# Five of 32 weight conversions moved into the first group's up projections, and the converted chunks of the second matrix stored by one request

## The chip, the cores and the metric

The kernel runs on one core of a Trainium2 chip. The metric is device time in microseconds (us) of one execution. The three runs of the kernel before took 1008.73, 1010.57 and 1010.68 us, median 1010.57 us.

## The reference, cut to what matters

```python
def reference(...):
    attn_out = _attn_ref(q, k, v)              # 4 x 8 heads x 576 x 64; keeps the 32 largest scores of each row
    x = attn_out.transpose(0, 2, 1, 3).reshape(2304, 512)
    h = x @ w_in                               # moe: 512 -> 2048
    g = np.maximum(h, 0.0) + alpha * np.minimum(h, 0.0)
    x = g @ w_out                              # 2048 -> 512
    return _moe2_ref(x, ...)                   # 8 experts, routed by w_gate, skip by w_skip
```

The inputs `w_in` and `w_out` arrive as 64-bit floats. The kernel reads them as pairs of 32-bit words and turns each weight into a high and a low 32-bit part, whose sum is the weight; every product of the two matrices is then three matmuls (high by high, high by low, low by high).

## The kernel before, in words

**Conversions.** Each matrix has 16 chunks of 128 x 512 weights: chunks 0 to 15 are of `w_in`, 16 to 31 of `w_out` (`convs`, line 285). `convert(i)` (line 287) takes the raw chunk (512 KB, loaded into half a `wr` buffer by `conv_load`, line 275) and issues three ScalarE (ACT) instructions, lines 297, 299 and 301. It hands back three later parts. `bits`, 4 slots on, is one VectorE (DVE) instruction of line 305, and then requests the raw chunk `i + 4`. `split`, 8 slots on, is two GpSimd (POOL) instructions, lines 311 and 112. `store`, 13 slots on, marks the chunk as converted and requests its store to DRAM on SP's queue, line 317 for `w_in` and 320 for `w_out` (there two requests, one for the high parts and one for the low, each in pieces of 512 bytes). The stores of chunks 28, 30 and 31 also call `fetch(0)`, `fetch(1)` and `fetch(2)` (line 322).

**Weights for the products.** `fetch(j)` (line 609) requests the 1 MB piece `j` of the converted weights from DRAM into a `wr` buffer, if `wr[j]` isn't held yet and its chunks are converted. There are three `wr` buffers, and the raw chunks use the same three, two chunks to a buffer (`cvtile`, line 266). A buffer is taken again when every instruction that reads it is done, and the request on SP's queue waits for that. `need(i)` (line 621) is called by the first product that uses piece `i`: it drops the pieces before `i` from `wr`, fetches `i` and `i + 1`, and a slot later `i + 2`.

**Order of the work.** Attention has 80 units (128 rows of a pair of heads; of five units of a pair the last has half the width). The loop of line 1277 makes one step `kx` per unit, in 14 slots. Line 23 (`STEP`) says what is issued in which slot: the fold of unit `kx + 1` on DVE (line 468) in slot 0; the values of unit `kx - 2` (line 569) and the scores of unit `kx + 2` (line 447) on TensorE (PE) in slot 1; copies of the scores by ACT (line 452) in slots 2 and 3; the DVE rounds (477, 480) in slots 2 to 8; the weights of the unit (510) in slots 10 and 11. The conversions and the MoE products come out of a list `todo`. Each slot adds a budget, and entries are issued while it is positive (`slot`, line 1113): a conversion costs 1.9, half an up projection of 128 features (six matmuls, line 644) 0.64. An entry that is a condition holds up all behind it. The budget of a step from `kx = 1` on is the cost of what is left divided by the steps until the next group is due, kept between 4.3 and 6.0, and half of it where the unit of half width comes next (lines 1293 to 1295).

**The first group.** `todo` begins with the first `EC` conversions (line 1140); `EC = 32`, all of them. At step 9, slot 8, the group of the first 256 rows is queued (`queue_moe`, line 1211): 16 up projections (features f0 to f15, 12 matmuls each), which use the pieces 0 to 7, two features each; then the downs (line 719) with the pieces 8 to 15. `queue_moe` mixes what is left in `convq` into this first group (lines 1237 to 1240): a conversion after every second entry, each behind the condition that the conversion two before it has been stored, at a cost of 0.5 instead of 1.9. With `EC = 32` nothing is left there. An up projection's result is taken from PSUM by ACT alone (663, 664) or, if issued in the slots 4 to 8 or among the last three, by ACT (686) and DVE (689).

Of the kernel before, what the change touches and what calls it, by code (L numbers as in the profile page):

```python
# [10 lines left out]
U16 = mybir.dt.uint16  # L11
AF = mybir.ActivationFunctionType
# [19 lines left out]
        (10, 0, "weights", 0), (10, -1, "evac", 2),  # L32
        (11, 0, "weights", 1)]
AHEAD = 4
EC = 32
PH = 6
RD = 3
WHOLE = ()
# [24 lines left out]
def kernel(  # L63
# [15 lines left out]
    nc = tc.nc  # L79
# [5 lines left out]
    KD = DM // 128  # L85
# [24 lines left out]
    def sub(o, a, b):  # L110

        behind_fold(nc.gpsimd.tensor_tensor(o, a, b, op=OP.subtract))  # L112
# [66 lines left out]
    for i in range(2):  # L179
        t = const.tile([128, 128], F32, name=f"vbd{i}")  # L180
# [41 lines left out]
    win_s = [dram.tile([128, 2, 2, 512], F32, name=f"win{j}") for j in range(KF // 2)]  # L222
    wout_s = [dram.tile([KD, 128, 8, 2, 128], F32, name=f"wout{j}") for j in range(KF // 8)]
# [42 lines left out]
    def cvtile(i):  # L266

        if i:
            return moe.tile([128, 1024], F32, name="cv", tag="g", bufs=8)
        if not ring:  # L270
            t = moe.tile([128, 16, 128], F32R, name="wr", tag="wr", bufs=3).rearrange("p a c -> p (a c)").bitcast(F32)
            ring.extend(t[:, h * 1024:(h + 1) * 1024] for h in range(2))
        return ring.pop(0)

    def conv_load(kind, f):
        raw = cvtile(0).bitcast(I32).rearrange("p (d f t) -> p d f t", d=4, t=2)
        if kind == 0:
            nc.sync.dma_start(
                raw.rearrange("p d f t -> p d (f t)"),
                win32[:, f * 256:(f + 1) * 256].rearrange("(d p) f -> p d f", p=128))  # L280
        else:
            nc.sync.dma_start(raw.rearrange("p d f t -> p (d f t)"), wout32[f * 128:(f + 1) * 128, :])
        raws[kind, f] = raw
# [3 lines left out]
    def convert(i):  # L287

        kind, f = convs[i]
        raw = raws.pop((kind, f))  # L290
        r2 = raw.rearrange("p d f t -> p (d f) t")
        hi, lo = r2[:, :, 1], r2[:, :, 0]
        hif = hi.bitcast(F32)
        w = cvtile(1).rearrange("p (a c) -> p a c", a=2)


        nc.scalar.activation(w[:, 0], hif, AF.Copy, scale=2.0 ** -112)
        t2 = w[:, 1].bitcast(U16).rearrange("p (c k) -> p c k", k=2)
        nc.scalar.activation(t2[:, :, 1].bitcast(mybir.dt.float16), hif, AF.Copy, scale=2.0 ** -60)
        top = raw.rearrange("p d f t -> p (d f t)").bitcast(U16).rearrange("p (c k) -> p c k", k=4)[:, :, 1]  # L300
        nc.scalar.activation(t2[:, :, 0], top, AF.Copy, scale=2.0 ** -13, bias=2.0 ** -14 - 0.5)

        def bits():
            t = w[:, 1].bitcast(I32)
            nc.vector.scalar_tensor_tensor(t, w[:, 0].bitcast(I32), 3, t, op0=OP.logical_shift_left,
                                           op1=OP.bitwise_or)
            if i + AHEAD < len(convs):
                conv_load(*convs[i + AHEAD])

        def split():  # L310
            nc.gpsimd.tensor_copy(w[:, 0].bitcast(F32R), w[:, 1])
            sub(w[:, 1].bitcast(F32R), w[:, 1], w[:, 0])

        def store():
            converted.add(i)
            if kind == 0:
                nc.sync.dma_start(win_s[f // 2][:, f % 2], w)
            else:
                for a in range(2):
                    nc.sync.dma_start(wout_s[f // 8][:, :, f % 8, a, :].rearrange("d p c -> p d c"),  # L320
                                      w[:, a].rearrange("p (d c) -> p d c", d=KD))
            if i in (28, 30, 31):
                fetch((28, 30, 31).index(i))

        if i == 0:
            return none + [bits, split] + none * (2 * CV) + [store]
        return none * (CV - 1 if i > 1 else 3 * CV) + [bits] + none * (CV - 1) + [split] + none * CV + [store]
# [281 lines left out]
    def fetch(j):  # L609
        if j < len(stream) and j not in wr and stream[j][1] in converted:  # L610
            wr[j] = wload(stream[j][0])
# [524 lines left out]
    def main(work, exact, hooks=(lambda: [], lambda: [], None)):  # L1136

        if not exact:
            convq.extend(lambda i=i: convert(i) for i in range(2 * KF))
            todo.extend((ECC, convq.pop(0)) for i in range(EC))  # L1140
            todo.insert(24, (0.5, late_consts))
            todo.insert(17, (0.5, late_loads))
# [68 lines left out]
        def queue_moe(wi):  # L1211
# [16 lines left out]
            if early[0]:  # L1228

                early[0] = False  # L1230
                mixed, k, n = [], EC, 0
                for p in parts:
# [107 lines left out]
    def place(n):  # L1340
        t = xtile(n).rearrange("p a n s -> p (a n s)")
        return t, [t[:, i * 2048:(i + 1) * 2048].rearrange("p (a c) -> p a c", a=2) for i in range(2)]
# [96 lines left out]
    t, two_ = place(0)  # L1439
# [3 lines left out]
    while todo or late or rowq:  # L1443
# [14 lines left out]
        if len(group[1]) == 2 and len(ups) == len(work) and gone > G2:  # L1458
            t, two_ = place(1)
# [168 lines left out]
```

## Time and profile before

| | |
|---|---|
| three runs | 1008.73, 1010.57, 1010.68 us |
| profiled execution, its own time | 1010.48 us |
| its span (first to last instruction) | 1008.7 us |
| busy: PE, DVE, ACT, POOL | 885.7, 797.6, 642.4, 399.1 us |
| mean granted clock of PE | 0.952 of full speed |

The profile is of one execution; times in it count from the first instruction. A busy share is the time in which an engine executes, not how well. The idle time in brackets in a timeline stands before the instruction named, with what ended it. The engines take their own instructions in order, so an instruction that waits holds up all behind it on that engine, and the same holds for SP's queue of transfers.

### The profile page before, as it was taken

The page shows a single profiled execution, that of the slowest core. Times are in us where ns is not written, and L with a number is a line of the kernel's source. Part 1 is how long each engine was busy: PE and PEld are TensorE (multiplying, and loading weights), DVE is VectorE, ACT ScalarE, POOL GpSimd, SP SyncE. Part 2 cuts the span into 40 slices and gives each one's busy share as a digit, 9 for nine tenths or more (in the row PEclk, how much of TensorE's full clock was granted, in tenths as well). Part 3 has the DMA queues.
Part 4 walks back from the last instruction along what each step waited for, and adds up shares of the span by engine and source line. Part 5 has one row for each costly group of instructions (what it writes and reads, how often), then busy time and mean ns, then how long its engine had stood idle before and what let it go on. Part 6 is the DMA issues. An engine that isn't in the chain of part 4 may idle for free. (4 is left out here: it accounts for less than half of the span.)

```text
span 1008.7 us, 21245 instructions
## 1 busy us (share of the span) xinstructions
PE 885.7 (88%) x7054; PEld 786.9 (78%) x7054; DVE 797.6 (79%) x2652; ACT 642.4 (64%) x1723; POOL 399.1 (40%) x608
## 2 busy tenths in 40 slices
PE   4345569999999999999999999999778989999995
PEld 2234458898999888999998899999668988987542
DVE  5999998999898799979987997999878532366410
ACT  7879768767865687588558857865456434365320
POOL 5866664522651254245213623541285134024100
PEclk9977579999999999999999999999797999999998
DMA  8978985776656566776656777665464679879993
GB/s 236 331 271 239 304 256 202 220 228 207 227 188 241 162 234 203 266 232 228 213 188 208 236 242 240 224 209 191 140 179 166 222 254 414 331 246 393 397 397 145
DMA packets 133319, 244.89 MB, mean 243 GB/s; under 512 B 58830, under 2 KB 91598, under 8 KB 116816
## 3 DMA queue, kind: packets, MB, share of 16 engines
q1 hardware_dynamic: 129824, 239.42, 70.0%
q0 software_dynamic: 2176, 3.73, 1.1%
q8 instruction: 58, 0.95, 0.4%
q14 instruction: 61, 0.50, 0.1%
q10 hardware_dynamic: 1200, 0.30, 0.1%
HBM read 215.00 MB, written 28.92 MB: 242 GB/s over the span
## 5 line engine op out<-in xcount | busy, mean ns | idle before, releaser
L644 PE MATMUL pm<-x,wr 128*128 128x256 f32 (+1 forms) x1536 | 245.6, 307 | 19.4 <-DVE ra L689 8.1
L719 PE MATMUL pm<-g,wr 128*128 128x256 f32 (+1 forms) x1536 | 235.5, 303 | 2.7 <-DVE ra L689 2.1
L644 PEld LDWEIGHTS pm<-x,wr 128*128 128x128 f32 x1536 | 213.3, 192 | 28.9 <-DVE ra L689 14.4
L719 PEld LDWEIGHTS pm<-g,wr 128*128 128x128 f32 x1536 | 208.8, 189 | 8.3 <-issue 4.0
L477 DVE MAX8 v<-F 128x8 f32<-128x72 f32 (+2 forms) x576 | 213.7, 407 | 1.2 <-issue 0.2
L112 POOL TENSOR_TENSOR g<-ra,g 128x256 fp32r<-128x256 f32 (+1 forms) x128 | 102.3, 820 | 150.2 <-DVE st L515 75.7
L510 DVE SCALAR_TENSOR_TENSOR Ex<-sb,v,Ex 128x577 f32<-128x577 f32 x144 | 130.9, 936 | 0.0
L480 DVE MATCH_REPLACE8 F<-v,F 128x72 f32<-128x72 f32 (+1 forms) x432 | 123.2, 291 | 0.0
L452 ACT ACTIVATE sb<-ps 128x288 f32<-128x288 f32 x224 | 80.2, 415 | 57.9 <-PE ps L447 46.2
L502 ACT ACTIVATE Ex<-sb,st 128x576 f32<-128x576 f32 x144 | 105.3, 782 | 0.1
L112 POOL TENSOR_TENSOR x<-xf,x 128x128 fp32r<-128x128 f32 (+1 forms) x80 | 40.2, 503 | 163.0 <-DVE st L515 113.9
L548 ACT ACTIVATE PT<-pt 128x512 f32<-128x512 f32 x144 | 86.9, 604 | 20.9 <-PE pt L536 20.2
L536 PE MATMUL pt<-ident,Ex 128*128 128x128 f32 x576 | 87.1, 284 | 4.3 <-ACT sb L452 4.3
L569 PE MATMUL px<-PT,vt 128*64 128x128 f32 (+1 forms) x1280 | 89.8, 288 | 0.0
L447 PE MATMUL ps<-kT,qT 64*128 64x288 f32 x576 | 80.2, 349 | 6.9 <-ACT kT L357 2.5
L689 DVE SCALAR_TENSOR_TENSOR ra<-ra,slope,pm 128x320 f32<-128x320 f32 (+1 forms) x69 | 35.5, 515 | 57.7 <-ACT ra L686 57.5
L569 PEld LDWEIGHTS px<-PT,vt 128*64 128x64 f32 x1280 | 70.6, 149 | 9.8 <-issue 2.0
L447 PEld LDWEIGHTS ps<-kT,qT 64*128 64x128 f32 x576 | 61.9, 212 | 20.6 <-issue 9.4
L536 PEld LDWEIGHTS pt<-ident,Ex 128*128 128x128 f32 x576 | 71.5, 147 | 6.7 <-ACT sb L452 6.0
L565 PE MATMUL px<-PT,vbd 128*128 128x128 f32 (+1 forms) x160 | 34.9, 302 | 39.3 <-ACT PT L553 37.4
L468 DVE TENSOR_TENSOR F<-m 128x144 f32<-128x144 f32 (+2 forms) x240 | 66.2, 329 | 0.0
L468 DVE TENSOR_TENSOR m<-sb 128x576 f32<-128x576 f32 (+1 forms) x80 | 64.8, 809 | 1.8 <-ACT sb L452 1.8
(379 smaller groups left out, 1558.9 us busy)
## 6 DMA issues: line engine op xcount, KB each, us to landing
wr<-win SPq DMA_DIRECT2D x64, 1024.0 KB, 5.0
wr<-wout SPq DMA_DIRECT2D x64, 1024.0 KB, 5.0
wd<-in_moe_w_dram SPq DMA_DIRECT2D x40, 512.0 KB, 11.4
wraw<-in_moe_w_dram SPq DMA_DIRECT2D x32, 512.0 KB, 7.1
wr<-in_moe_w_in_dram SPq DMA_DIRECT2D x16, 512.0 KB, 5.7
vt<-in_v_dram SPq DMA_DIRECT2D x32, 256.0 KB, 2.8
win<-cv SPq DMA_DIRECT2D x16, 512.0 KB, 4.9
wr<-in_moe_w_out_dram SPq DMA_DIRECT2D x16, 512.0 KB, 5.5
```

Source lines behind the costliest of these rows:

```text
L112: behind_fold(nc.gpsimd.tensor_tensor(o, a, b, op=OP.subtract))
L447: nc.tensor.matmul(self.ps[h, j][:, 0:HALF], lhsT=hd["q"][gp, a, u * 128 - hd["c0"]:(u + 1) * 128 - hd["c0"]], rhs=hd["k"][gp, b_, c0:c0 + ...
L468: gate[0] = nc.vector.tensor_tensor(o[:, n_], a[:, n_, 0:w], a[:, n_, w:2 * w], op=op)
L477: nc.vector.max(v8[:, h, r, :], F[:, h, 0:w])
L480: nc.vector.match_replace(out=F[:, h, 0:w], in_to_replace=v8[:, h, r, :], in_values=F[:, h, 0:w], imm_value=NEG)
L502: nc.scalar.activation(self.Ex[:, h, :], self.sb[:, h, :], AF.Exp, bias=self.st[:, 0, h:h + 1], scale=0.125)
L510: nc.vector.scalar_tensor_tensor(self.Exp[:, cs], self.sbp[:, cs], v8[:, h, 3, 7:8], self.Exp[:, cs], op0=OP.is_ge, op1=OP.mult, accum_out ...
L536: nc.tensor.transpose(pt[:, c * 128:(c + 1) * 128], P[:, c0:c0 + 128], ident)
L548: nc.scalar.activation(PT[:, 4 * h:4 * h + 4, :].rearrange("p a b -> p (a b)"), pt, AF.Copy)
L569: nc.tensor.matmul(x[h * 64:(h + 1) * 64, 0:n], lhsT=hd["vt"][:, h, c, :], rhs=rhs, start=False, stop=(c == SF - 1))
L644: nc.tensor.matmul(hp[:, 0:n], lhsT=w[:, (f % 2) * 8 + a * 4 + d, :], rhs=x[:, d, c0:c1], start=(i == 0), stop=(i == 3 * KD - 1))
L719: nc.tensor.matmul(op_[:, 0:n], lhsT=w[:, 2 * f + a, :], rhs=g[(hf + ch) * 8 + f, sg][:, gg, 0:n], start=(i == 0), stop=(i == ni - 1))
```

## The change

`EC` is 27: the conversions 27 to 31 (the last five chunks of `w_out`) are left in `convq`, and `queue_moe` mixes them in among the first up projections. A converted chunk of `w_out` is laid out with the high and low parts of each quarter side by side (the three ACT instructions, the one of DVE and the two of POOL address it in four runs), and stored by one request in pieces of 1 KB, in place of two requests in pieces of 512 bytes.

```diff
-EC = 32
+EC = 27
...
         kind, f = convs[i]
         raw = raws.pop((kind, f))
-        r2 = raw.rearrange("p d f t -> p (d f) t")
-        hi, lo = r2[:, :, 1], r2[:, :, 0]
+        hi = raw[:, :, :, 1]
         hif = hi.bitcast(F32)
-        w = cvtile(1).rearrange("p (a c) -> p a c", a=2)
+        t4 = cvtile(1)
+        w = t4.rearrange("p (d a c) -> p a d c" if kind else "p (a d c) -> p a d c", a=2, d=4)
...
-        t2 = w[:, 1].bitcast(U16).rearrange("p (c k) -> p c k", k=2)
-        nc.scalar.activation(t2[:, :, 1].bitcast(mybir.dt.float16), hif, AF.Copy, scale=2.0 ** -60)
-        top = raw.rearrange("p d f t -> p (d f t)").bitcast(U16).rearrange("p (c k) -> p c k", k=4)[:, :, 1]
-        nc.scalar.activation(t2[:, :, 0], top, AF.Copy, scale=2.0 ** -13, bias=2.0 ** -14 - 0.5)
+        t2 = w[:, 1].bitcast(U16).rearrange("p d (c k) -> p d c k", k=2)
+        nc.scalar.activation(t2[:, :, :, 1].bitcast(mybir.dt.float16), hif, AF.Copy, scale=2.0 ** -60)
+        top = raw.rearrange("p d f t -> p d (f t)").bitcast(U16).rearrange("p d (c k) -> p d c k", k=4)[:, :, :, 1]
+        nc.scalar.activation(t2[:, :, :, 0], top, AF.Copy, scale=2.0 ** -13, bias=2.0 ** -14 - 0.5)
...
             if kind == 0:
-                nc.sync.dma_start(win_s[f // 2][:, f % 2], w)
+                nc.sync.dma_start(win_s[f // 2][:, f % 2], t4.rearrange("p (a c) -> p a c", a=2))
             else:
-                for a in range(2):
-                    nc.sync.dma_start(wout_s[f // 8][:, :, f % 8, a, :].rearrange("d p c -> p d c"),
-                                      w[:, a].rearrange("p (d c) -> p d c", d=KD))
+                nc.sync.dma_start(wout_s[f // 8][:, :, f % 8].rearrange("d p a c -> p d a c"),
+                                  t4.rearrange("p (d a c) -> p d a c", a=2, d=4))
             if i in (28, 30, 31):
                 fetch((28, 30, 31).index(i))
```

## Rows read from the trace of the kernel before

**Rows 1.** Stages: window, length, busy (count) of PE, PEld, DVE, ACT, POOL, PEclk, DMA share, GB/s.
```profile
41.10:138.60 97.50, 51.15 (x313) 40.87 (x313) 97.47 (x281) 80.11 (x187) 64.89 (x70) 0.69 0.85 258
146.40:157.70 11.30, 10.88 (x78) 10.05 (x79) 8.47 (x34) 6.63 (x22) 2.89 (x7) 0.70 0.72 251
...
199.00:206.80 7.80, 7.80 (x79) 7.41 (x78) 7.80 (x31) 5.46 (x16) 2.13 (x5) 1.00 0.43 140
...
168.90:237.50 68.60, 65.57 (x622) 61.32 (x623) 67.66 (x248) 50.48 (x157) 27.06 (x47) 1.00 0.67 218
237.50:700.00 462.50, 452.46 (x3999) 426.02 (x3999) 421.20 (x1505) 329.02 (x959) 175.47 (x268) 1.00 0.66 219
```

**Rows 2.** Timeline of DVE: start, us, what. A step begins with m<-sb.
```profile
138.63 0.85 DVE L468 TENSOR_TENSOR m<-sb 128x288 f32<-128x288 f32 x1
...
146.38 1.00 DVE L468 TENSOR_TENSOR m<-sb 128x576 f32<-128x576 f32 x1
...
152.13 0.28 DVE L576 TENSOR_TENSOR xf<-px,R 128x128 f32<-128x128 f32 x1
...
157.29 0.48 DVE L689 SCALAR_TENSOR_TENSOR ra<-ra,slope,pm 128x256 f32<-128x256 f32 x1 [2.83 <-ACT ra L686]
...
166.58 0.46 DVE L468 TENSOR_TENSOR m<-sb 128x288 f32<-128x288 f32 x1
```

**Rows 3.** DVE: line 305 at 41.1 to 138.6 (min/median/max ns).
```profile
L305 DVE SCALAR_TENSOR_TENSOR cv<-cv x23: 666/685/1750, 40.1 to 137.3; 128x512 int32<-128x512 int32 x23
```

**Rows 4.** DVE groups, the first fold: at 25 to 150 us, then at 200 to 300 us.
```profile
L468 DVE TENSOR_TENSOR m<-sb 128x576 f32<-128x576 f32 x10 | 12.9, 1285 | 0.0
...
L468 DVE TENSOR_TENSOR m<-sb 128x576 f32<-128x576 f32 x10 | 7.8, 782 | 0.0
```

**Rows 5.** ACT: group of line 297 at 25 to 150 us (busy, mean ns, idle before).
```profile
L297 ACT ACTIVATE cv<-wr 128x512 f32<-128x512 f32 x26 | 17.9, 687 | 0.0
```

**Rows 6.** Timeline of ACT.
```profile
135.91 0.68 ACT L297 ACTIVATE cv<-wr 128x512 f32<-128x512 f32 x1
...
137.11 0.78 ACT L301 ACTIVATE cv<-wr 128x512 uint16<-128x512 uint16 x1
...
144.29 0.19 ACT L485 ACTIVATE st<-v 128x1 f32<-128x1 f32 x1
...
151.64 1.13 ACT L452 ACTIVATE sb<-ps 128x288 f32<-128x288 f32 x3 [1.94 <-PE ps L447]
...
164.28 0.59 ACT L548 ACTIVATE PT<-pt 128x512 f32<-128x512 f32 x1
```

**Rows 7.** Timeline of PE.
```profile
146.81 1.44 PE L644 MATMUL pm<-x,wr 128*128 128x256 f32 x5 [2.12 <-POOL x L112]
148.05 0.63 PE L565 MATMUL px<-PT,vbd 128*128 128x128 f32 x2
...
150.51 1.33 PE L447 MATMUL ps<-kT,qT 64*128 64x288 f32 x7
...
163.88 3.11 PE L644 MATMUL pm<-x,wr 128*128 128x256 f32 x24
166.82 0.33 PE L565 MATMUL px<-PT,vbd 128*128 128x64 f32 x2
...
169.86 0.44 PE L372 MATMUL ps<-ident,nat 128*128 128x128 f32 x2 [1.10 <-ACT sb L452]
```

**Rows 8.** SP's queue at 145 us; and, of tile wr at 120 to 200 us, landing times.
```profile
145.07 13.65 SPq L591 DMA_DIRECT2D wr<-win  x3
...
DMA to landing us min/median/max: 4.8/5.0/8.0
```

**Rows 9.** DMA issues of the page: count, KB each, median us to landing.
```profile
wr<-win SPq DMA_DIRECT2D x64, 1024.0 KB, 5.0
...
win<-cv SPq DMA_DIRECT2D x16, 512.0 KB, 4.9
...
wout<-cv SPq DMA_DIRECT2D x32, 256.0 KB, 4.1
```

## The prediction

> **What bounds the kernel now.** First I read the stages. From 41.1 to 138.6 us (steps 1 to 8) DVE is busy 97.47 of 97.50 us and PE only 51.15: this stretch, in which the conversions run, is DVE's. In step 10 (146.4 to 157.7) neither is full. From 168.9 to 237.5, the rest of the first group, DVE is busy 67.66 of 68.6 us and PE 65.57; from 237.5 to 700 PE is busy 452.46 of 462.5 [rows 1]. So up to step 21 (237.5) DVE sets the pace with PE close behind, and then PE does, with a fixed amount of work ahead. What the change makes of the start of step 21 stays to the end. Next, DVE's timeline: the only large hole is 2.83 us at 154.46, where DVE waits for ACT and ACT for an up projection [rows 2]. A step without conversions lasts 7.80 us [rows 1]; eight last 62.4, the stretch 97.5, so its 22 conversions (the x23 of [rows 3] less the one at 40.1) cost 35.1/22 = 1.6 us each. Lines 245 to 250 ran there too; I take **1.5 us**, though the instruction itself has a median of 0.685 [rows 3].
>
> So a conversion that is moved within DVE's stretch gains nothing by being moved. What can be gained are holes: 2.83 us in step 10 and about 1 us of 68.6 later.
>
> **The change, step by step.** *Fewer conversions in the head.* At step 1, 18 of the budget is spent (1.95, 8 and 8 in steps -2, -1 and 0). Of 32 x 1.9 + 1 = 61.8 that leaves 43.8 for eight steps, 5.5 a step; of 27 x 1.9 + 1 = 52.3 it leaves 34.3, 4.3 a step. Either list ends with step 8, and counted slot by slot 31 `bits` were issued by then and 27 will be. Four times 1.5: step 9 starts **6.0 us earlier**, at 132.6 for 138.63 [rows 2].
>
> *What is issued instead.* Step 9, slot 8: conversion 27; slot 11: the first half of f0. Step 10: second half of f0 in slot 0, conversion 28 in slot 2, conversion 29 (it needs the store of 27, 13 slots after it) and f1 in slot 7. Step 11: conversion 30 in slot 1, conversion 31, f2 and f3 in slot 6, f4 and half of f5 in slots 10 and 11. By step 12, slot 0, 6 of 16 up projections are issued, where it was 8. The group is done at step 21, slot 0, instead of step 20, slot 11; the next group starts at step 21 either way.
>
> *The wait that is added.* Before, pieces 0 to 2 were fetched by the stores of chunks 28, 30 and 31, ahead of f0. Now the first call is f0's own `need(0)`. All three `wr` buffers then hold raw chunks (26 and 27; 28 and 29; 30 and 31), so piece 0 waits for ACT to finish conversion 27, piece 1 for 29, piece 2 for 31, in this order on SP, with the stores and the q, k and v loads queued behind. SP standing still there is no new thing (13.65 us at 145.07 [rows 8]), but then the pieces were already in.
>
> *Price at f0.* ACT reaches slot 8 after line 485 at 144.29, 5.8 us into step 9 [rows 6], so at 138.4; the three instructions take 137.89 - 135.91 = 2.0 us [rows 6]; request at 140.5; landing 5.0 us (4.8 to 8.0 [rows 8]): 145.5. PE, idle until then, runs f0's 12 matmuls at the low pace of [rows 7], 5 in 148.05 - 146.81 = 1.24 us, so 3.0 us: 148.5. Values 2.46 and 1.13 to the first copy of scores (148.05 to 150.51 to 151.64 [rows 6, 7]): 152.1. Then ACT, in order: two copies 0.75, conversion 28 2.0: 154.8. DVE stands at `bits` 28 in slot 6 of step 10, where it arrives at 132.6 + 13.5 = 146.1 (152.13 - 138.63 [rows 2]). **DVE idles some 8.7 us**, and is done at 155.5, where it had passed at 152.13: 3.4 us late. The lead is gone.
>
> *Steps 10 and 11.* The rest of step 10 takes 2.3 (152.13 to 154.46), `bits` 29 1.5, line 689 of f1 0.4 and a wait for ACT, which has conversion 29 first, between 0 and the 2.83 of [rows 2]; I take 0.7. Step 11 starts at 160.4, not 157.7 [rows 1]. It had 8.9 us (157.7 to 166.58) and gets `bits` 30 and 31, 3.0, and one more line 689, 0.4: step 12 starts at 172.7, **6.1 us late**. Two more of line 689 fall into later steps (10 up projections instead of 7 are issued in slots that use it): 7.0.
>
> In these steps the durations of DVE depend on POOL. The fold of 128 x 576 takes 1285 ns in the head and 782 later [rows 4], and `bits` up to 1750 ns against 666 [rows 3]; the slow ones go with the stretch in which POOL does the splits. The Trainium skill (SBUF — State Buffer, Who interferes with whom) says that a DVE instruction with two SBUF inputs and a GpSimd instruction that reads SBUF exclude each other for a whole instruction; these rows agree, and by that rule a conversion costs its 1.5 us wherever POOL splits it. By the instruction alone, 0.68, the sum would be 2.5 us lower (three times 0.8).
>
> *Price on PE.* Conversion 31 starts on ACT about 6.6 us into step 11 (164.28 - 157.7 [rows 1, 6]), 167.0, ends at 169.0; piece 2 lands at 174.0. f4 waits for it. f4 and f5 at the full pace (24 in 166.82 - 163.88 = 2.94 us [rows 7]): 176.9; values and scores of step 12 another 2.0: 178.9. Before, PE was there at 169.86 - 1.10 = 168.8 [rows 7]: 10.1 late, and it owes two projections, 2.9. Its idle time up to step 21 was 68.6 - 65.57 = 3.0 [rows 1]. If all of that is filled, it ends **10.0 us late**.
>
> *What costs nothing.* The stores: one request of 512 KB for two of 256 KB; the nearest rows land in 4.9 and 4.1 us [rows 9]. Nobody waits for them in the head, since ACT was never idle ahead of line 297 [rows 5]; 0, at most a few tenths either way. The four runs of 128 in the conversions' addresses: the first fold, in two runs, takes 782 ns for 576 elements, `bits` 685 for 512, the same for an element [rows 3, 4]; 0, with 0.1 us either way. Two more loads: the stores of 30 and 31 come in step 12 (slots 0 and 5), after f4 and f6 (step 11, slot 10; step 12, slot 4) have dropped pieces 1 and 2; `fetch(1)` and `fetch(2)` load them again, for nobody. Each holds a `wr` buffer for 5.0 us; between 0 and 5 us together, and I take 0, since pieces 3 and 4 are asked for ahead of them.
>
> *Sum.* DVE's books say 7.0, PE's 10.0, and the later should win unless PE loses less than I think; I take 8.5. On the profiled execution's own 1010.48 us (0.1 below the median) that is **1019.0 us**.
>
> **Rivals.** A measurement of this kernel can tell about 0.2%, 2.0 us, from no change.
>
> 1. *The hole is covered* (faster). The lead of 6.0 us meets no long wait: f0 finds its weights soon enough, DVE does the moved work in the hole that it had. Gained are the 2.83 and about 1 us of holes and what POOL no longer costs, four times 0.8 less 1.3 of line 689: some 5.5 us, 1005.0. For it: a DVE without slack in the head and a hole in step 10. Against: piece 0 can't be requested before conversion 27 is through ACT. It decides at a landing of piece 0 by 136.8 (145.5 less the 8.7 of the hole).
> 2. *A wash.* The wait for piece 0 eats the lead and PE, behind by two projections, catches up while DVE sets the pace of steps 12 to 20: 1010.5, within 2. Against: 3.0 us of idle PE is too little for 13.
> 3. *It compounds* (slower still). Landing takes 8.0 us at pieces 0 and 2, when stores and raw chunks share the engines, and the two idle loads delay f10: 8.5 + 3 + 5, 1027.
> 4. *It isn't what it says.* The conversions sit among the first two of 16 projections only, and two pieces are loaded twice. This is in the sum and has no chance of its own.
>
> **Numbers.** Forecast 0.55 (own range 1013 to 1024), rival 3 0.12, wash 0.13, covered 0.20. That gives faster 0.20, same 0.13, slower 0.67. For 8 in 10 I leave out the outer half of the covered case and of the compounded one: 1005 to 1027.
>
> **What would show it.** After: `wr<-win` x66 instead of x64; `wout<-cv` x16 of 512 KB; step 9 near 132.6; PE waiting near 136 to 146 for a DMA of `wr<-win`, not for POOL; DVE idle over 5 us ahead of line 305 in step 10; step 12 near 172.7 and step 21 near 246. I am wrong if DVE has no such hole, if step 21 starts before 237, or if PE after 237 makes up for a late start.

## The result, and the profile after

The changed kernel takes **1023.32 us** (median of four runs, 1022.55 to 1023.98); the kernel before, over four runs, 1010.15 (1008.73 to 1010.68). The ratio is **1.0128, interval 1.0116 to 1.0141**: slower by 13.2 us. The profiled execution took 1023.89 us, its span is 1022.1 (1008.7 before, so 13.4 longer) and the mean granted clock 0.947 (0.952). All line numbers of the changed kernel from 316 on are one lower than before.

First the stages, cut where the steps of the changed kernel begin (columns as in [rows 1]): step 10, step 11, the rest of the first group, and what follows.

```profile
138.50:156.10 17.60, 8.96 (x67) 7.89 (x67) 9.73 (x35) 8.97 (x25) 6.00 (x9) 0.81 0.27 86
156.10:167.60 11.50, 8.35 (x60) 7.65 (x60) 11.50 (x36) 8.89 (x22) 6.58 (x8) 0.83 1.04 363
167.60:246.70 79.10, 74.05 (x679) 69.58 (x679) 70.78 (x262) 53.68 (x163) 29.30 (x49) 0.94 0.74 255
246.70:700.00 453.30, 443.21 (x3910) 417.50 (x3908) 411.34 (x1475) 322.44 (x937) 174.20 (x265) 0.99 0.66 220
```

Step 10 lasts 17.6 us instead of 11.3 [rows 1], and in it PE is idle for half of the time, DVE for 7.9 us, and the DMA engines move little (share 0.27). Every engine waits for another there, in a chain. In the rest of the group both engines have holes, 5.1 us on PE and 8.3 on DVE (3.0 and 0.9 in [rows 1]), and the granted clock of PE is 0.94, where it was 1.00. It was at the lower of its two levels in two stretches. The first began 0.5 us after a wait of PE of 3.15 us had ended, the second within one of 3.76 (at f4 and f10, below):

```profile
167.10:170.40 3.30, 3.30 (x18) 3.30 (x17) 3.16 (x16) 1.48 (x4) 1.11 (x1) 0.50 1.04 436
187.60:194.30 6.70, 5.85 (x33) 5.33 (x34) 4.03 (x24) 0.81 (x3) 3.24 (x5) 0.50 0.94 333
```

After 246.7 PE has no more idle time than before, 10.1 us (462.5 - 452.46 = 10.0 in [rows 1]); what is lost there all the same is told further down.

DVE's timeline of the changed kernel shows the same steps as [rows 2]; a step begins with m<-sb.

```profile
131.14 0.45 DVE L467 TENSOR_TENSOR m<-sb 128x288 f32<-128x288 f32 x1
...
138.47 0.75 DVE L467 TENSOR_TENSOR m<-sb 128x576 f32<-128x576 f32 x1
...
150.56 0.69 DVE L305 SCALAR_TENSOR_TENSOR cv<-cv 128x512 int32<-128x512 int32 x1 [6.51 <-ACT cv L301]
...
154.37 0.81 DVE L305 SCALAR_TENSOR_TENSOR cv<-cv 128x512 int32<-128x512 int32 x1 [0.87 <-ACT cv L301]
155.67 0.48 DVE L688 SCALAR_TENSOR_TENSOR ra<-ra,slope,pm 128x256 f32<-128x256 f32 x1 [0.49 <-ACT ra L685]
156.07 0.75 DVE L467 TENSOR_TENSOR m<-sb 128x576 f32<-128x576 f32 x1
...
163.80 1.75 DVE L509 SCALAR_TENSOR_TENSOR Ex<-sb,v,Ex 128x577 f32<-128x577 f32 x1
...
165.48 0.68 DVE L305 SCALAR_TENSOR_TENSOR cv<-cv 128x512 int32<-128x512 int32 x1
166.08 0.86 DVE L688 SCALAR_TENSOR_TENSOR ra<-ra,slope,pm 128x256 f32<-128x256 f32 x2
...
167.60 0.45 DVE L467 TENSOR_TENSOR m<-sb 128x288 f32<-128x288 f32 x1
```

The lead of the lighter head (the stretch up to step 8) is there: step 9 starts 7.5 us earlier (131.14 for 138.63), step 10 7.9. Then DVE stands for 6.51 us ahead of `bits` of conversion 28, and again for 0.87 and 0.49. Of 7.9 us of lead 1.6 are left at step 11, and step 12 is 1.0 late (167.60 for 166.58). PE and SP's queue say why. PE, with f0, then f2 and f3, f4 and f5, and f10:

```profile
142.66 2.93 PE L643 MATMUL pm<-x,wr 128*128 128x256 f32 x12 [7.79 <-DMA wr<-win]
...
160.03 3.21 PE L643 MATMUL pm<-x,wr 128*128 128x256 f32 x24
...
166.61 4.62 PE L643 MATMUL pm<-x,wr 128*128 128x256 f32 x24 [3.15 <-DVE ra L688]
...
188.45 2.90 PE L643 MATMUL pm<-x,wr 128*128 128x256 f32 x12 [3.76 <-DVE v L476]
```

SP's queue (start, how long the issue took, buffer waits included); 1024 KB of `wr<-win` is one piece:

```profile
137.85 15.95 SPq L590 DMA_DIRECT2D wr<-win  x2
153.85 0.42 SPq L282 DMA_DIRECT2D wr<-in_moe_w_out_dram  x1
154.37 0.38 SPq L590 DMA_DIRECT2D wr<-win  x1
...
163.53 1.37 SPq L590 DMA_DIRECT2D wr<-win  x2
...
171.26 0.32 SPq L590 DMA_DIRECT2D wr<-win  x1
...
180.67 4.38 SPq L590 DMA_DIRECT2D wr<-win  x3
```

Piece 0 goes out at 137.85, as soon as conversion 27 is through ACT, and f0 starts when it has landed, 4.8 us later, at 142.66. Piece 1 then holds up SP until 153.4, and all that stands behind it on SP. The second long wait of PE, 3.15 us at f4, is not for a piece: piece 2 landed at 163.06, and the wait ends with line 688. The third, at f10, is put down to line 476, but piece 5, which f10 uses, was requested at 181.11 and landed 7.2 us later, at 188.3, and f10 starts at 188.45; the runs below show the same. The transfers, with KB and the median us to landing:

```profile
wr<-win SPq DMA_DIRECT2D x66, 1024.0 KB, 5.4
...
wout<-cv SPq DMA_DIRECT2D x16, 512.0 KB, 5.0
```

66 pieces instead of 64 and 16 stores instead of 32 [rows 9]: the change does what its diff says. The two pieces too many, loaded again for nobody, I call the **idle loads**; they are those of 171.26 and the first of 180.67.

### The profile page after: what moved, and what is told of

Same layout as the page of the kernel before. It is cut to its first block, busy times and chain, and to the rows that moved or that the text cites. A ratio compares the mean times of both kernels' runs of the same rounds, so it can differ in the third digit from the quotient of the medians.

```text
span 1022.1 us, 21208 instructions
## 1 busy us (share of the span) xinstructions
PE 892.0 (87%) x7054; PEld 791.7 (77%) x7054; DVE 794.7 (78%) x2655; ACT 642.8 (63%) x1720; POOL 392.5 (38%) x605
## 5 line engine op out<-in xcount | busy, mean ns | idle before, releaser
L643 PE MATMUL pm<-x,wr 128*128 128x256 f32 (+1 forms) x1536 | 249.2, 311 | 28.8 <-DMA wr<-win 11.3
L643 PEld LDWEIGHTS pm<-x,wr 128*128 128x128 f32 x1536 | 217.4, 196 | 38.0 <-DVE ra L688 14.4
L476 DVE MAX8 v<-F 128x8 f32<-128x72 f32 (+2 forms) x576 | 214.2, 408 | 1.1
L112 POOL TENSOR_TENSOR x<-xf,x 128x128 fp32r<-128x128 f32 (+1 forms) x80 | 41.1, 514 | 169.9 <-DVE st L514 106.6
## 6 DMA issues: line engine op xcount, KB each, us to landing
wr<-win SPq DMA_DIRECT2D x66, 1024.0 KB, 5.4
wr<-wout SPq DMA_DIRECT2D x64, 1024.0 KB, 5.0
wd<-in_moe_w_dram SPq DMA_DIRECT2D x40, 512.0 KB, 11.5
vt<-in_v_dram SPq DMA_DIRECT2D x32, 256.0 KB, 2.8
```

Source lines behind the costliest of these rows:

```text
L476: nc.vector.max(v8[:, h, r, :], F[:, h, 0:w])
L643: nc.tensor.matmul(hp[:, 0:n], lhsT=w[:, (f % 2) * 8 + a * 4 + d, :], rhs=x[:, d, c0:c1], start=(i == 0), stop=(i == 3 * KD - 1))
```

## The experiments

Each is compared with runs of the kernel before on its own chip (medians between 1009.57 and 1010.02 us). The table has the start of the fold of a step in each profiled execution (one for each kernel), as the difference to the kernel before, in us; a minus is a lead.

| kernel | step 10 | 11 | 12 | 13 | 15 | 21 | 23 | 33 | 74 | span |
|---|---|---|---|---|---|---|---|---|---|---|
| the change | -7.9 | -1.6 | +1.0 | +3.2 | +7.4 | +9.2 | +10.9 | +11.0 | +13.9 | +13.4 |
| e1 | 0.0 | -1.3 | -1.3 | -1.3 | -1.3 | -1.3 | -1.3 | -1.3 | -1.7 | -1.3 |
| e2 | -7.4 | -0.7 | +1.9 | +4.1 | +8.7 | +10.5 | +12.2 | +12.3 | +15.1 | +14.7 |
| e3 | -7.2 | -0.3 | +2.3 | +4.5 | +4.0 | +5.8 | +7.6 | +8.9 | +8.7 | +10.4 |
| e4 | -7.7 | -8.7 | -6.1 | -3.7 | -1.5 | +0.3 | +2.1 | +3.3 | +3.4 | +4.4 |
| e5 | -7.7 | -8.7 | -6.1 | -3.2 | -3.7 | -2.0 | -0.3 | +1.0 | +0.8 | +1.4 |
| e6 | -7.4 | -8.3 | -4.9 | -5.3 | -5.8 | -4.1 | -2.3 | +0.4 | +1.6 | +2.9 |
| e7 | -1.8 | -1.2 | -0.5 | -1.0 | -1.8 | -0.5 | -0.4 | +0.7 | +0.7 | -0.7 |
| e8 | -7.5 | -0.5 | +4.7 | +5.1 | +4.7 | +6.5 | +8.2 | +9.4 | +10.1 | +9.5 |
| e9 | -2.1 | -3.7 | -3.7 | -4.3 | -5.1 | -3.7 | -3.7 | -3.7 | -3.7 | -6.2 |
| e10 | +0.1 | +2.6 | +2.6 | +2.6 | +2.6 | +2.6 | +2.6 | +4.2 | +5.0 | +2.3 |

The theory: the head gives some 7 us, and the pieces that are now requested on demand, while raw chunks hold their buffers, take it back and more; the idle loads add to that. The rivals: the loss lies in the layout and the store; the moved conversions cost it by themselves; the condition that lets a conversion pass only after a store holds the up projections up.

**The two halves of the change.** The first run keeps the new layout and store and converts all 32 in the head, the second changes `EC` alone, in the kernel before.

The diff of e1 against the changed kernel, then of e2 against the kernel before:

```diff
-EC = 27
+EC = 32
```

```diff
-EC = 32
+EC = 27
```

> All 32 conversions stay in the head; only the new layout and the single request of 1 KB pieces are kept. Theory (the loss comes from the five moved conversions): 1010 us, within 1.5 of the kernel before. Rival (the addressing in four runs or the new store costs or gains something itself): outside that; 1015 or more if each of the 16 chunks lost 0.3 us on ACT, VectorE and GpSimd, 1007 or less if the head had been held by its stores.

> The five conversions are moved, with the old layout and the two requests of 512-byte pieces. Theory: as the changed kernel, 1023, within 1.5. Rival (layout or store matter): the difference to 1023 is what they give or cost with the move in place.

Measured: e1 1010.55 us, ratio **1.0004** (0.9987 to 1.002); e2 1023.48, ratio **1.0116** (1.0089 to 1.0143). The layout and the store cost nothing that can be measured, the move costs all of it. The store of e1 in the view of transfers, beside `x32, 256.0 KB, 4.1` of [rows 9]:

```profile
wout<-cv SPq DMA_DIRECT2D x16, 512.0 KB, 4.5
```

Half as many requests and pieces twice as large: 512 KB land in 4.5 us, 256 KB in 4.1, and the end does not move. The first rival falls.

**Without the idle loads.** The changed kernel without the two lines that fetch pieces when 28, 30 and 31 are stored.

```diff
-            if i in (28, 30, 31):
-                fetch((28, 30, 31).index(i))
```

> The changed kernel without the call of fetch in the stores of 28, 30 and 31, so that pieces 1 and 2 are loaded once: 64 loads of wr from win, not 66. Theory: the two idle loads hold back piece 5 and with it f10, for which TensorE stood 3.8 us at 185 us; that wait goes, steps 15 to 17 lose nothing more, 4 to 6 us less than 1023: 1018. Rival (the loss is the moved VectorE work alone, and the idle loads are hidden): 1023, within 1.

Measured: 1019.94 us, ratio **1.008** (1.0055 to 1.0105), where the change has 1.0128: 3.4 us less, a little under the 4 to 6 that I expected. PE, at f0 and at f4:

```profile
143.37 2.93 PE L641 MATMUL pm<-x,wr 128*128 128x256 f32 x12 [7.48 <-DMA wr<-win]
...
167.92 4.57 PE L641 MATMUL pm<-x,wr 128*128 128x256 f32 x24 [3.47 <-DVE ra L686]
```

Both waits stay; the one at f10 is gone. From step 13 to 15 this kernel gains 0.5 us where the change loses 4.2, and at step 21 it is 3.4 us better. So the wait at f10 was made by the idle loads: the first took the buffer that came free at 171.26, the second waited for the next one until 180.67, and piece 5 stood behind it on SP until 181.11. "DVE v L476" in the row of f10 is what happened to end at that moment.

**Pieces 0 and 1 early.** The half of the buffers for x that only the second batch uses is free here. Piece 0 (e4), or 0 and 1 (e5), goes there ahead of f0, so nothing is requested on demand at f0; the second argument of `wload` names the place. The diff is of e5, which has no idle loads either; e4 fetches piece 0 alone, at the store of 24, and keeps the old lines.

```diff
-            if i in (28, 30, 31):
-                fetch((28, 30, 31).index(i))
+            if i in (23, 24):
+                fetch(i - 23)
...
-            wr[j] = wload(stream[j][0])
+            wr[j] = wload(stream[j][0], j if j < 2 and not exact_[0] else None)
```

> The changed kernel, with piece 0 of the weights in memory of its own (the half of x that the second batch uses later), loaded when chunk 24 is stored, so that f0 no longer waits for it. The two idle loads stay (or one of them). Theory: TensorE starts f0 when its x is there, about 8 us into step 9 instead of 11.5; VectorE's hole of 6.5 us ahead of bits 28 shrinks to 2 to 3, and step 12 starts 3 to 5 us earlier, before 165: 1018 to 1020. Rival (VectorE's moved work sets the pace of steps 10 to 12 in any case, the hole is only where the slack shows): step 12 as late as now, 1022 to 1024.

> The changed kernel with pieces 0 and 1 in the half of x that the second batch uses later, loaded when chunks 23 and 24 are stored, and without the calls of fetch in the stores of 28, 30 and 31: neither f0 nor f2 waits for weights, no piece is loaded twice. Theory: with piece 0 alone step 12 started 6.1 us ahead of the kernel before, and the rest was lost again at f4 (5.2 us, both PSUM banks taken in one slot), at the idle loads (2.9) and by 1.8 in steps 21 and 22; without the idle loads 3 of these come back: step 21 2 to 4 us ahead, 1009 to 1012. Rival (what was won by step 12 is lost again by the pace of steps 12 to 20 whatever the loads do): 1013 to 1015, as with piece 0 alone.

Measured: e4 1013.77 us, ratio **1.0038** (1.0019 to 1.0056); e5 1011.86, ratio **1.0015** (1.0001 to 1.0028). For e4 I had expected 1018 to 1020, so the late piece 0 was worth more than I thought. In e4 the `bits` at which DVE stood for 6.51 us has no idle time before it:

```profile
144.16 0.68 DVE L305 SCALAR_TENSOR_TENSOR cv<-cv 128x512 int32<-128x512 int32 x1
```

The lead of 7.7 us passes step 10 untouched. What is left is lost later: PE of e4 at f4 and at f10:

```profile
159.50 4.91 PE L649 MATMUL pm<-x,wr 128*128 128x256 f32 x24 [5.23 <-DVE ra L694]
...
180.76 2.90 PE L649 MATMUL pm<-x,wr 128*128 128x256 f32 x12 [2.87 <-DMA wr<-win]
```

The wait at f10, with the idle loads still in, is now named as what it is, a transfer. The wait at f4 is longer than in the change: with piece 0 in time it comes into sight.

**The wait at f4.** f2 and f3 are issued in one slot and fill both PSUM buffers for up projections. Each is freed by DVE (line 688), and this stands in DVE's order behind `Ex` (line 509) and `bits` of conversion 31 (165.48 to 166.08 in the timeline of DVE above); f4 starts at 166.61, when the first of the two is done. They are issued together because the condition ahead of them, "the conversion two before is stored", comes true late. Here e5 gets another condition: the raw chunk has been requested.

```diff
-                        mixed.append((lambda i=k - 2: i in converted, None))
+                        mixed.append((lambda i=k: convs[i] in raws, None))
```

> As the run before, but a mixed conversion waits only until its raw chunk has been requested, not until the conversion two before it is stored. So f1 to f3 are not held up for a step and then issued in a heap. Theory (the wait by stores makes TensorE late by two projections and fills both PSUM banks at f2 and f3): the 5.2 us ahead of f4 go, the group is done as early as in the kernel before: 1003 to 1008. Rival (the five conversions then come so close together that ACT is late with the copies of the scores, and VectorE has its hole again): 1010 or more.

> The changed kernel without the idle loads, and with the mixed conversions waiting only for their raw chunk. Piece 0 is still requested at f0, after conversion 27. Theory: VectorE's hole ahead of bits 28 stays (6 to 7 us), the 3.5 us at f4 and the lag of two projections go: 1014 to 1017, against 1020 without the idle loads alone. Rival (the lag and f4 are followers of the late piece 0, not of the wait by stores): 1019 to 1021.

Measured: e6 (on e5) 1008.66 us, ratio **0.9991** (0.9973 to 1.0009), a little above what I expected; e8 (the same on e3, piece 0 on demand) 1019.75, ratio **1.0093** (1.0058 to 1.0128), where the rival's 1019 to 1021 held and my 1014 to 1017 missed. PE of e5 at f4 and f5 (24 matmuls); PE of e6 at f4 (two rows) and at f5; then PE of e8 at f0 and at f2:

```profile
159.50 5.37 PE L651 MATMUL pm<-x,wr 128*128 128x256 f32 x24 [5.23 <-DVE ra L696]
```

```profile
155.07 0.98 PE L651 MATMUL pm<-x,wr 128*128 128x256 f32 x6 [1.28 <-ACT low L671]
156.02 0.95 PE L651 MATMUL pm<-x,wr 128*128 128x256 f32 x6
...
159.80 1.70 PE L651 MATMUL pm<-x,wr 128*128 128x256 f32 x12 [2.83 <-DVE ra L696]
```

```profile
143.19 2.93 PE L641 MATMUL pm<-x,wr 128*128 128x256 f32 x12 [7.56 <-DMA wr<-win]
...
159.50 1.65 PE L641 MATMUL pm<-x,wr 128*128 128x256 f32 x6 [3.42 <-DMA wr<-win]
```

In e6 f4 starts at 155.07, 4.4 us sooner than in e5, after 1.28 us of idle time; 2.83 us more are idle ahead of f5, 4.1 together for 5.23. f4 and f5 are done at 161.5, in e5 at 164.9, and the lead at step 15 is 5.8 for 3.7. In e8 the condition buys nothing: f2, which comes sooner, waits 3.42 us for its piece, which is as late as ever. The condition is the second cause and shows only when the first is gone.

**Three conversions fewer to move.** The changed kernel with `EC = 30`, then e6 with it.

```diff
-EC = 27
+EC = 30
```

> The changed kernel with EC = 30: two conversions are moved instead of five. Piece 0 is then requested by the store of chunk 28, half a step ahead of f0, and its buffer is free, and no piece is loaded twice. Theory (the loss is the request on demand, the heap at f4 and the idle loads): none of the three, 1009 to 1012. Rival (every moved conversion costs the same, 13/5 = 2.6 us): 1015.

> EC = 30 with pieces 0 and 1 loaded early into the half of x that the second batch uses later, no idle loads, and the mixed conversions waiting only for their raw chunk: the version that should lose nothing. Theory: no wait for weights at f0 (4.8 us with EC = 30 alone), no heap; VectorE 3 us ahead at step 9 and its hole in step 10 gone, but TensorE has a fixed amount of work from step 21 on, and with EC = 27 a lead of 4.1 us at step 21 was worth nothing at the end: 1005 to 1009. Rival (every lead in the head is worth itself at the end): 1003 or less.

Measured: e7 1011.30 us, ratio **1.0017** (1.0002 to 1.0033); e9 1008.82, ratio **0.9992** (0.998 to 1.0004). PE and DVE of e7:

```profile
144.39 2.93 PE L643 MATMUL pm<-x,wr 128*128 128x256 f32 x12 [4.76 <-DMA wr<-win]
```

```profile
153.26 0.69 DVE L305 SCALAR_TENSOR_TENSOR cv<-cv 128x512 int32<-128x512 int32 x1 [3.06 <-ACT cv L301]
```

My expectation that f0 would not wait missed: piece 0 is requested at 138.05, and f0 starts 6.3 us later. But DVE's hole, 3.06 us, is then hardly larger than the 2.83 that the kernel before has at line 689 [rows 2], and there are no idle loads, so little is lost. e9 kept a lead of 3.7 us from step 11 to 74 in its profiled execution, its fastest (1004.34 us); its eleven runs reach up to 1011.52, and the median does not differ from before by what can be measured. None of these versions beats the kernel before.

**The kernel before, on demand.** The lines that fetch pieces 0 to 2 early are taken out of the kernel before; no conversion is moved.

```diff
-            if i in (28, 30, 31):
-                fetch((28, 30, 31).index(i))
```

> The kernel before, without the calls of fetch in the stores of 28, 30 and 31, so that f0's own call is the first request of piece 0, though all conversions are done by then and a buffer is free. Theory (a request on demand is dear in itself, since it stands on SP behind the last stores and TensorE waits with all of attention behind it): piece 0 lands at 147 to 151 instead of ahead of f0, f0 ends 2 to 5 us later, 1011 to 1014. Rival (it is dear only where a conversion holds the buffer): 1010, within 1.

Measured: 1015.89 us, ratio **1.0061** (1.0042 to 1.008), above the 1011 to 1014 that I expected. PE at f0, and DVE at the end of step 10:

```profile
148.85 2.93 PE L642 MATMUL pm<-x,wr 128*128 128x256 f32 x12 [6.49 <-DMA wr<-win]
```

```profile
159.87 0.48 DVE L687 SCALAR_TENSOR_TENSOR ra<-ra,slope,pm 128x256 f32<-128x256 f32 x1 [3.27 <-ACT ra L684]
```

A piece on demand costs by itself: the kernel before, whose conversions all end in the head, loses 6 us by it. In the table it loses 2.6 at step 11, at f0, and 2.4 more by step 74, of which 1.6 between steps 23 and 33 go with the granted clock (last section); that execution was the fastest of its four (1012.80), so the rest of the 6 us is not in this trace.

**The sum by runs.** From the change (1.0128) to e3 (1.0080) 4.8 thousandths, the idle loads; to e5 (1.0015) 6.5, pieces 0 and 1 early; to e6 (0.9991) 2.4, the condition. Some 4.8, 6.6 and 2.4 us of the 1010; each of the ratios has an interval of 1 to 3 thousandths on either side, and the first difference is 3.6 if e2, run beside e3 on one chip, stands for the change. With all three mended the move neither gains nor loses that can be measured.

## Why the prediction was right, and which steps were off

Direction and range were right, the mechanism at f0 too; 1019.0 was 4.3 us short. Up to step 21 terms of both signs were mis-sized and nearly cancelled; the 4.3 us came after step 21, where I had put nothing ("What the change makes of the start of step 21 stays to the end").

**Fewer conversions in the head.** Predicted 6.0 us for four, measured 7.5 (7.1 in e2, 7.0 in e3): 1.7 to 1.9 each, not 1.5. Most of it comes from the neighbours of a conversion on DVE. `Ex` (line 510) in steps 1 to 8 before (41.1 to 138.6 us), then in the changed kernel (line 509, 41.0 to 131.1), with busy time and mean ns:

```profile
L510 DVE SCALAR_TENSOR_TENSOR Ex<-sb,v,Ex 128x577 f32<-128x577 f32 x16 | 18.2, 1165 | 0.0
```

```profile
L509 DVE SCALAR_TENSOR_TENSOR Ex<-sb,v,Ex 128x577 f32<-128x577 f32 x16 | 14.9, 957 | 0.0
```

That is 3.3 of the 7.5 us; the first two folds of a step give 2.1 (17.5 us before, 15.4 after) and line 305 itself 1.7 (19.6 and 17.9). My 1.5 was a mean over all 22; the four that went were worth more.

**What is issued instead**, and step 21 as the start of the next group: right.

**Price at f0.** The place was right in each link: request when conversion 27 is through ACT, landing in about 5 us (4.8), f0 at the low pace (2.93 us for 12), scores, copy, conversion 28, DVE's hole at `bits` 28. The sizes were not: the hole was predicted at 8.7 us and measured at 6.51. The request went out at 137.85 and not at 140.5. DVE left `bits` 28 at 151.25, 0.9 us ahead of the kernel before, and not 3.4 behind.

**Steps 10 and 11.** I priced the moved conversions at 1.5 us each, for POOL splits beside them. The four have:

```profile
L305 DVE SCALAR_TENSOR_TENSOR cv<-cv x4: 681/734/810, 150.6 to 165.5; 128x512 int32<-128x512 int32 x4
```

Only one neighbour was doubled, `Ex` at 163.80, 1.75 us where it takes 0.80 at 152.69, while POOL ran line 112 (163.67 to 164.93). With its 0.95 the four cost about 1.0 each. Beside the `Ex` at 152.69 it was POOL's line 112, begun after it (152.81), that took longer, 1.82 us for some 1.27. The Trainium skill (SBUF — State Buffer, Who interferes with whom) states that a DVE instruction with two SBUF inputs and a GpSimd one that reads SBUF contend. These rows agree, and so does the first fold of step 9 (0.85 us before, beside line 311 on POOL, 0.45 with POOL idle); my use of it, the full price wherever there is a split, was too much. Step 12 was predicted 6.1 us late and was 1.0 late: that DVE was done with `bits` 28 at 151.25 and not at 155.5 is 4.3 of the 5.1.

**Price on PE.** That f4 waits was right, for what was not. I had piece 2 wait for conversion 31 and land at 174.0. It was requested at 154.37, with the buffer of conversions 28 and 29, and landed at 163.06. Piece 1 ahead of it had not waited for conversion 29, as I had it, but for piece 0's own buffer: it was requested at 153.47, when f1 was done (153.43). So the three buffers did not come in turn here. f4 waited instead for line 688 behind `bits` 31; e6, which lets the entries pass sooner, cut the idle time ahead of f4 and f5 from 5.23 to 4.1. I had also put f4 and f5 at the full pace, 2.94 us; after the wait, with the granted clock at 0.50 for most of them, they took 4.62. What "PE owes" was right: at step 21 the downs are not through. Matmuls of the downs in steps 20 and 21, in the changed kernel (each row: window, length, PE busy and count, PEld busy and count, clock, DMA share, GB/s), then in the kernel before:

```profile
238.15:246.66 8.51, 6.05 (x45) 5.35 (x44) 1.00 0.61 247
246.66:256.12 9.46, 1.32 (x11) 1.11 (x10) 1.00 0.62 224
```

```profile
228.99:237.50 8.51, 4.86 (x35) 4.13 (x34) 1.00 0.60 234
237.50:246.20 8.70, 0.00 (x0) 0.00 (x0) 1.00 0.54 171
```

Step 20 is as long in both and does ten more, and eleven more run in step 21. Between steps 21 and 23 every kernel with `EC = 27` loses the same 1.8 us, with a late start (the change) or an early one (e6, from -4.1 to -2.3); e7 and e9 lose nothing. It is in the order of the work and not in the waits: e6, 4.1 us ahead at step 21, has x45 in step 20 and x12 in step 21 as well. I had this term inside PE's books of 10.0 at step 21; it falls due two steps later, on top of the 9.2 measured there.

**What costs nothing.** The store and the layout: right (e1). The two idle loads: this is **the step that failed**. I bounded them by 0 and 5 us and took 0, "since pieces 3 and 4 are asked for ahead of them". They are; piece 5 is not. The price was not the 5.0 us in which each holds a buffer, but the time that the second stood on SP for one, with piece 5 behind it. f10 then ran its 12 matmuls in 2.90 us, at the granted clock of 0.50, where 12 took 1.70 at full clock (f5 of e6). e3 puts the two loads at 3.4 us at step 21, and the ratios at 3.6 to 4.8 thousandths. With the upper end the sum would have been 1024.0.

**Sum.** Step 21 "near 246" came true (246.66) by luck, by errors against each other: step 12 was 5.1 us better than I had it, and from there to step 21 the kernel lost 8.2 us where I had 2.4. Of the 8.2, 2.2 fall to f4 (steps 12 to 13), 4.2 to f10 (steps 13 to 15) and 1.8 to steps 15 to 21, where every kernel with `EC = 27` loses 1.6 to 1.8. That PE, once it sets the pace, makes up for nothing was right; that the start of step 21 stays to the end was not. 1.8 us fell due by step 23, and from there to the end of the span the changed kernel loses 2.5 us more, in steps of 0.5, 1.3 and 1.1 us around steps 53, 62 and 72. At the second of these the granted clock was at its lower level, and in the kernel before it was not. The changed kernel, then the kernel before in the same part of the work (11.5 us earlier):

```profile
627.90:631.20 3.30, 3.30 (x17) 3.30 (x18) 0.01 (x2) 1.29 (x4) 1.14 (x1) 0.50 0.50 114
```

```profile
616.40:619.70 3.30, 3.08 (x26) 2.82 (x25) 0.00 (x0) 2.60 (x7) 1.44 (x2) 1.00 0.52 119
```

At the other two, low stretches lie near in both kernels, and what they lost is not shown. Why the clock fell in one kernel and not in the other stays open.

**Rivals.** Rival 3 had half of it, the idle loads that delay f10, without the landing of 8.0 us at piece 0 (4.8; piece 2 did take 8.7, but f4 did not wait for it). Rival 1, the covered hole, was wrong for this change by its own condition (landing by 136.8; it was 142.6). e6 builds its case, and gives 1008.66 us and not 1005.0: of the lead of 4.1 us at step 21, 1.8 is work still owed, and its profiled execution, the slowest of its ten (1013.43), loses 2.7 more by step 33 with the granted clock (last section). The wash was wrong.

## What to carry to other kernels

When work is moved behind a point at which a transfer is requested, look at what the buffers hold at that point: here raw chunks held all three, and a landing of 5 us became 8 us of idle PE and most of a lead of 7.5, because each engine in turn stood in its own order behind it. After two of the long waits PE ran at the lower clock as well (24 matmuls in 4.62 us for 2.94 at full pace), so that these waits cost more than their length. A request that nobody needs is not free for having a buffer: it stands in the queue ahead of one that somebody needs. And a lead at a step counts only with the work that is done by then; compare the counts of matmuls, not the starts of steps alone.

## What the runs showed that I had not expected

The same four transposes took 0.66 us or 1.12, with the same 0.69 us of idle PE before them. First the kernel before, then e7, each with the stage around them (columns as in [rows 1]):

```profile
342.93 0.66 PE L807 MATMUL pm<-ident,x2t 128*128 128x128 f32 x4 [0.69 <-ACT xr L812]
...
341.70:348.40 6.70, 4.57 (x37) 3.82 (x35) 3.38 (x16) 4.37 (x13) 0.32 (x1) 1.00 0.52 178
```

```profile
342.44 1.12 PE L806 MATMUL pm<-ident,x2t 128*128 128x128 f32 x4 [0.69 <-ACT xr L811]
...
341.70:348.40 6.70, 5.32 (x25) 4.73 (x25) 2.89 (x15) 4.56 (x14) 0.52 (x1) 0.50 0.56 186
```

The granted clock tells the two apart: 1.00 in the one and 0.50 in the other. e3 to e8 and e10 lose 1.2 to 2.7 us between steps 23 and 33, where these stand; in each of the seven the clock is at its lower level there, for 6.8 to 10.2 us, and the transposes take 1.11 or 1.12 us. In the kernel before, the change, e1, e2 and e9 it is not, and they lose none. Which of the two a kernel gets followed neither its lead nor its lag, so it can hide or feign a gain of this size. PE stands for 0.69 us twice there in all of them; what makes the clock fall in some was not tried. The runs of one kernel spread by as much, 1004.34 to 1011.52 us in e9; whether the clock is behind that is not shown, as only one execution of each kernel was traced.
